# Attention scores masked by TensorE, minima by one VectorE instruction out of PSUM, exponentials straight from there

## The chip, the cores and the metric

The kernel runs on one core of one Trainium2 chip. The time is the device time of the program in microseconds (us). Engines are named as in the profile: PE is TensorE (PEld its weight loads), DVE is VectorE, ACT is ScalarE, POOL is GpSimd, SP is SyncE, which here issues most transfers.

## The reference, cut to what matters

The program is one attention layer, then a mixture of eight experts with one expert per token, then a two-layer product with a squared ReLU. The change touches the attention (and the sums of squares of its result, which the router needs):

```python
def _attn_ref(q, k, v):                        # 4 batches, 8 heads, 576 positions, 64 wide
    scores = scale * np.matmul(q, k.transpose(0, 1, 3, 2))      # scale = 1/8
    mask = (rel >= 0) & (rel < 64)             # a query sees itself and the 63 before it
    scores = np.where(mask, scores, -1e9)
    scores = scores - np.max(scores, axis=-1, keepdims=True)
    attn = np.exp(scores)
    attn = attn / (np.sum(attn, axis=-1, keepdims=True) + 1e-09)
    return np.matmul(attn, v)

def _moe_ref(x, ...):                          # x: 2304 tokens, 512 wide
    xn = x / (np.linalg.norm(x, axis=-1, keepdims=True) + 1e-06)
    logits = xn @ en.T / tau                   # argmax picks the expert, softmax gives the gate
    ...
```

## The kernel before, in words

**Steps.** The result of attention has 2304 rows, taken as 18 tiles of 128 tokens (t = 0 to 17). A tile holds two blocks of 64 queries (c = 0, 1), and a block needs 128 keys: its own 64 and the 64 before. Heads go in four pairs (hp); the two heads of a pair lie in the two halves of the partitions. `steps` is a list of 36 steps, each with two slots (t, hp). A step makes 2 slots x 2 heads x 2 blocks of scores, in a PSUM tile `spb` of two banks, one for each head: `spb[128, head, n % 2, slot, 128]`. The halves n % 2 alternate from step to step, and both lie in the same bank.

**Order.** PE's and SP's order is written by hand (the loop at L873): scores of step n, then pieces of `prep` (transposes of q and k for later steps), the flips of step n-2 (transposes of its exponentials), router work that is due (`run`), and the products with v of step n-3 (`fins`, and one step sooner from step 31 on). DVE, ACT and POOL are ordered by a planner that simulates the program; waits between engines follow from which instruction reads and writes which tile.

**One step's softmax.** `scores` (L234): 16 matmuls write q times k; four DVE instructions, one for each slot and head, add a mask from SBUF, scale by -1/8, write the sum to `sm` in SBUF and keep its minimum in `mn`. In steps 2 to 30 POOL then subtracts the minimum, and one ACT instruction takes exp(-x) over all 512 columns (L252, L259); in the others ACT makes four exponentials with the minimum as bias (L262). `flip` (L265) transposes by PE and copies back by ACT; `pv` (L273) multiplies with v, and DVE divides by the row sums (L283 to L289).

**Preparation.** `prep` (L216) turns k and q of one unit (a batch and a pair of heads) by PE into PSUM; each of its four pieces is copied out by two instructions, on ACT for both heads of k and head 0 of q, on DVE for head 1 of q (`TOACT`, L770). There are 16 units, so 64 pieces.

**Router.** When a tile's last product is done, `fin` (L656) puts on the list: the write of the tile to memory, `route_turn` (transposes, a copy by ACT, and the sum of squares, L379 to L383: by ACT for tiles below 16, by DVE for the last two), logits, and some steps later ranks, lists, `route_norm` on POOL (L449) and gates. `x2p` holds a buffer `xh` that the first expert's tokens use later.

Of the kernel before, what the change touches and what calls it, by code (L numbers as in the profile page):

```python
# [8 lines left out]
F32 = mybir.dt.float32  # L9
# [11 lines left out]
def tile_kernel(ctx, tc, q, k, v, emb, tau, w1, w2, w_in, w_out, s_in, b_in, out, x_dram, y_dram, y0_dram, wi_dram, wo_dram):  # L21
# [7 lines left out]
    QC = S // (2 * QP)  # L29
    BIG = 3.0e38  # L30

# [161 lines left out]

    mask = at.tile([128, 3, 128], F32, name="mask")
    nc.gpsimd.memset(mask, 0.0)
    for v_ in range(3):
        for h in range(2):
            m = mask[64 * h:64 * h + 64, v_]
            if v_ == h + 1:
                nc.gpsimd.affine_select(out=m, in_=m, compare_op=ALU.is_ge, fill=-8.0e9,  # L200
                                        base=0, pattern=[[-1, 128]], channel_multiplier=1)
                continue
            nc.gpsimd.affine_select(out=m, in_=m, compare_op=ALU.is_ge, fill=-8.0e9,
                                    base=-1, pattern=[[1, 128]], channel_multiplier=-1)
            nc.gpsimd.affine_select(out=m, in_=m, compare_op=ALU.is_ge, fill=-8.0e9,
                                    base=64, pattern=[[-1, 128]], channel_multiplier=1)

# [8 lines left out]
    def prep(b, hp):  # L216

        kt, qt = qk.pop((b, hp))
        n = (b * NP + hp) % NB
        for nm, src, dst in (("k", kt, kTs[n]), ("q", qt, qTs[n])):  # L220
            for h in range(2):
                pt = ps3.tile([128, QC, QP], F32, tag="tp", name="tp")
                for c in range(QC):
                    nc.tensor.transpose(pt[:, c], src[:, h, c], ident[:QP, :QP])
                for par in range(2):
                    o = dst[64 * h:64 * h + 64].rearrange("r (c p e) -> r e c p", c=QC, e=2)[:, par]
                    i = pt[64 * par:64 * par + 64]
                    if (nm, h) in TOACT:
                        nc.scalar.activation(o, i, AF.Copy)
                    else:  # L230
                        nc.vector.tensor_copy(o, i)
                yield

    def scores(n, slots):  # L234
        for s, (t, hp) in enumerate(slots):
            for c in range(2):
                u, i = unit(t, hp, c)
                k0 = max(i - 1, 0) * 64
                for h in range(2):
                    rows = slice(64 * h, 64 * h + 64)  # L240
                    nc.tensor.matmul(spb[64 * c:64 * c + 64, h, n % 2, s], qTs[u][rows, i * 64:i * 64 + 64],
                                     kTs[u][rows, k0:k0 + 128], start=True, stop=True)
        sm = at3.tile([128, 4, 128], F32, tag="sm", name="sm")
        mn = at3.tile([128, 4], F32, tag="mn", name="mn")
        for s, (t, hp) in enumerate(slots):
            m = mask[:, 1 if 2 * t % NW == 0 else 2 if (2 * t + 1) % NW == 0 else 0]
            for h in range(2):
                j = 2 * s + h
                nc.vector.tensor_tensor_reduce(out=sm[:, j], in0=spb[:, h, n % 2, s], in1=m, scale=-1.0 / 8.0,
                                               scalar=BIG, op0=ALU.add, op1=ALU.min, accum_out=mn[:, j:j + 1])  # L250
        if P0 <= n < PS:
            nc.gpsimd.tensor_tensor(sm, sm, mn.unsqueeze(2).to_broadcast([128, 4, 128]), op=ALU.subtract)  # L252
            return sm, None
        return sm, mn

    def exps(sm, mn):
        pe = at3.tile([128, 4, 128], F32, tag="pe", name="pe")
        if mn is None:
            nc.scalar.activation(pe, sm, AF.Exp, scale=-1.0)  # L259
            return pe  # L260
        for j in range(4):
            nc.scalar.activation(pe[:, j], sm[:, j], AF.Exp, bias=mn[:, j:j + 1], scale=-1.0)  # L262
        return pe
# [49 lines left out]
    zer = rp.tile([128, 1], BF16, name="zer")  # L313

    def add(out, a, b):
        nc.tensor.matmul(out, a, b, start=False, stop=True, skip_group_check=True)

# [53 lines left out]
    def route_turn(t, lp=None):  # L371
# [5 lines left out]
        marks.append(nc.scalar.activation(xt, tp, AF.Copy))  # L377
        sq = (lp or at).tile([128, DM], F32, tag="sq", name="sq")
        if t >= TL:  # L379
            nc.vector.tensor_tensor_reduce(out=sq, in0=xw, in1=xw, scale=1.0, scalar=0.0,  # L380
                                           op0=ALU.mult, op1=ALU.add, accum_out=ss[:, t:t + 1])
        else:
            nc.scalar.activation(sq, xw, AF.Square, accum_out=ss[:, t:t + 1])  # L383
        return xt

    def route_logits(t, xt):
        for c in range(ND):
            for o in range(0, 128, 64):
                add(lg[o:o + 64, t], xt[:, c, o:o + 64], enT[:, c])

    def block(kk, ln, a):
# [264 lines left out]
    def fin(slots, pT):  # L656
# [4 lines left out]
        ts_ = sorted({t for t, _ in slots})  # L661
        nt = len(ts_)

        def write():
# [104 lines left out]
    now = [0]  # L769
    TOACT = (("k", 0), ("k", 1), ("q", 0))  # L770

# [63 lines left out]

    P0, PS = 2, 31

# [457 lines left out]
```

## Time and profile before

| | |
|---|---|
| time | 839.34 us median of 3 runs (836.24 to 839.41) |
| profiled execution | 840.44 us, its span 838.7 us, mean granted clock 0.964 |
| PE busy | 788.7 us (94%), 6350 matmuls |
| DVE, ACT, POOL busy | 507.8 us (61%), 393.9 us (47%), 203.5 us (24%) |

The attention stage is the first 156 us or so of the span; the experts and the last products follow. PEclk of the page is the TensorE clock that was granted, as a share of 2.4 GHz; 0.5 is 1.2 GHz. Busy time counts an engine as busy while an instruction of it runs; an instruction's idle time before it stands in brackets with what ended it. The copies of exponentials back from PSUM have L270, the q and k copies L229 (ACT) and L231 (DVE).

### The profile page before, as it was taken

Reading aid. Unit: us, or ns where it says so; the run is one execution under the profiler, and the core shown is the slowest. Engines: PE = TensorE matmul, PEld = TensorE weight load, DVE = VectorE, ACT = ScalarE, POOL = GpSimd, SP = SyncE. Lnnn points to the kernel's source line nnn. Section 1 sums busy time; section 2 is a strip of 40 time slices with the busy share of each in tenths; the row PEclk is TensorE's granted clock in tenths of the full one; section 3 lists DMA queues with packets and bytes.
Section 4 is the critical chain, followed back from the end, with each engine's and each line's share of the span. In section 5 each row is a group of like instructions: output and inputs, shape, how many; then the busy total and the mean of one; then the engine's idle time right before and its main releaser. Section 6 shows DMA issues by size and latency. Waiting matters only on the chain.

```text
span 838.7 us, 16564 instructions
## 1 busy us (share of the span) xinstructions
PE 788.7 (94%) x6350; PEld 722.9 (86%) x6350; DVE 507.8 (61%) x1306; ACT 393.9 (47%) x796; POOL 203.5 (24%) x188
## 2 busy tenths in 40 slices
PE   6988887698999999899899999999999999999996
PEld 4776776598999999899899999999999999999885
DVE  3746586867777658689565555666655444444442
ACT  5866877414434545446354444445535333322331
POOL 3412335431112352444202222222210110101010
PEclk9967996889999999999899999999999999999999
DMA  8954846136849778677463332333324111100000
GB/s 186 216 150 125 217 131 213 73 119 201 238 154 317 230 250 270 219 243 273 163 218 111 101 101 101 100 114 107 121 89 124 53 38 39 51 26 26 27 26 26
DMA packets 100643, 117.16 MB, mean 140 GB/s; under 512 B 38885, under 2 KB 72165, under 8 KB 100561
## 3 DMA queue, kind: packets, MB, share of 16 engines
q1 hardware_dynamic: 91072, 99.11, 39.2%
q0 software_dynamic: 3232, 10.24, 3.5%
q10 hardware_dynamic: 6256, 6.72, 2.4%
q8 instruction: 51, 0.84, 0.4%
q14 instruction: 32, 0.25, 0.1%
HBM read 91.52 MB, written 24.53 MB: 138 GB/s over the span
## 4 chain that ended last, share of the span: by engine, by line
PE 50%; issue 0%; DMA 0%; POOLq 0%; DVE 0%
PE p L126 49%; PE tp L132 1%; DMA out_dram<-o,ids 0%; POOLq L1290 0%; DVE o L1240 0%; POOLq L1241 0%
## 5 line engine op out<-in xcount | busy, mean ns | idle before, releaser
L126 PE MATMUL p<-xl,wh 128*128 128x256 f32 x576 | 162.6, 282 | 0.0
L126 PE MATMUL p<-xh,wh 128*128 128x256 f32 x576 | 162.3, 282 | 0.0
L126 PE MATMUL p<-xh,wl 128*128 128x256 f32 x576 | 161.9, 281 | 0.0
L1202 ACT ACTIVATE r<-p 128x256 f32<-128x256 f32 x144 | 55.2, 384 | 168.5 <-PE p L126 162.3
L1203 DVE SCALAR_TENSOR_TENSOR r<-r,s_bc 128x256 f32<-128x256 f32 x144 | 79.5, 554 | 79.2 <-ACT r L1202 78.9
L126 PE MATMUL p<-wh,gh 128*128 128x512 f32 x288 | 113.1, 393 | 0.0
L126 PE MATMUL p<-wl,gh 128*128 128x512 f32 x288 | 113.1, 393 | 0.0
L126 PE MATMUL p<-wh,gl 128*128 128x512 f32 x288 | 113.0, 393 | 0.0
L126 PEld LDWEIGHTS p<-xh,wh 128*128 128x128 f32 x576 | 108.9, 189 | 0.7
L126 PEld LDWEIGHTS p<-xl,wh 128*128 128x128 f32 x576 | 108.7, 189 | 0.8
L126 PEld LDWEIGHTS p<-xh,wl 128*128 128x128 f32 x576 | 109.1, 189 | 0.0
L1026 POOL TENSOR_TENSOR fl<-fl,fs 128x512 f32<-128x512 f32 x32 | 45.9, 1438 | 253.1 <-DVE fs L1025 215.6
L88 DVE TENSOR_TENSOR wl<-raw,wh 128x1024 fp32r<-128x1024 f32 x72 | 102.5, 1432 | 7.0 <-ACT wh L87 6.9
L87 ACT ACTIVATE wh<-raw 128x1024 fp32r<-128x1024 f32 x80 | 83.3, 1056 | 7.9 <-DMA raw<-in_moe_w_dram 3.8
L126 PE MATMUL p<-hh,wh 128*128 128x256 f32 (+5 forms) x256 | 78.7, 308 | 0.0
L126 PE MATMUL p<-hl,wh 128*128 128x256 f32 (+5 forms) x256 | 77.0, 301 | 0.0
L126 PE MATMUL p<-hh,wl 128*128 128x256 f32 (+5 forms) x256 | 77.0, 301 | 0.0
L1209 ACT ACTIVATE gh<-r,b_bc 128x256 fp32r<-128x256 f32 x144 | 72.5, 503 | 7.4 <-DVE r L1203 7.4
L1210 DVE SCALAR_TENSOR_TENSOR gl<-r,b_bc,gh 128x256 fp32r<-128x256 f32 x144 | 71.2, 494 | 3.1 <-ACT gh L1209 3.1
L1241 POOL DMA_INDIRECT out_dram<-o,ids x18 | 18.6, 1035 | 203.7 <-DVE o L1240 182.5
L126 PEld LDWEIGHTS p<-wh,gl 128*128 128x128 f32 x288 | 54.1, 188 | 12.1
L126 PEld LDWEIGHTS p<-wh,gh 128*128 128x128 f32 x288 | 54.1, 188 | 11.4
(222 smaller groups left out, 1488.7 us busy)
## 6 DMA issues: line engine op xcount, KB each, us to landing
raw<-in_moe_w_dram SPq DMA_DIRECT2D x64, 512.0 KB, 4.8
raw<-y_dram SPq DMA_DIRECT2D x18, 512.0 KB, 3.8
vb<-in_v_dram SPq DMA_DIRECT2D x64, 128.0 KB, 3.7
fr<-in_moe_w_in_dram SPq DMA_DIRECT2D x16, 512.0 KB, 5.6
fr<-in_moe_w_out_dram SPq DMA_DIRECT2D x16, 512.0 KB, 4.2
k<-in_k_dram SPq DMA_DIRECT2D x32, 144.0 KB, 3.4
q<-in_q_dram SPq DMA_DIRECT2D x32, 144.0 KB, 3.6
x_dram<-xs SPq DMA_DIRECT2D x8, 512.0 KB, 3.2
```

What stands on the lines that cost most here:

```text
L87: a = nc.scalar.activation(hi, src, AF.Copy)
L88: return a.ins, le.tensor_tensor(lo, src, hi.bitcast(F32), op=ALU.subtract).ins
L126: nc.tensor.matmul(ps, a[x], b[y], start=first and j == 0, stop=last and j == 2)
L132: nc.tensor.matmul(ps, x, y, start=j == 0, stop=j == len(k) - 1)
L1026: nc.gpsimd.tensor_tensor(lf, lf, sg.bitcast(F32), op=ALU.mult)
L1202: nc.scalar.activation(r, ps, AF.Relu)
L1203: nc.vector.scalar_tensor_tensor(r, r, s_bc, r, op0=ALU.mult, op1=ALU.mult)
L1209: nc.scalar.activation(gh, r, AF.Identity, bias=b_bc)
L1210: nc.vector.scalar_tensor_tensor(gl, r, b_bc, gh.bitcast(F32), op0=ALU.add, op1=ALU.subtract)
L1241: nc.gpsimd.indirect_dma_start(out=out, out_offset=bass.IndirectOffsetOnAxis(ap=ids[:, k:k + 1], axis=0), in_=o, in_offset=None)
```

## The change

- The mask becomes a bf16 tile of 0 and 1e9. Before a step's score matmuls, PE writes it into PSUM with four matmuls by an identity of 64 (one for each block and head, 256 columns each), and the score matmuls add to it. The scale -1/8 is put on q when it is copied out of PSUM in `prep`.
- One DVE `tensor_reduce` takes the minima of all 512 columns of the step from PSUM. `sm` and POOL's subtraction go.
- ACT makes four exponentials of 128 columns in every step, reading the scores from PSUM with the minimum as bias.
- All q copies are on DVE (`TOACT` keeps k).
- The squares of tiles 0 to 10 are no longer ACT's: when a group of one or two tiles is done, `squares` on POOL multiplies it by itself and adds halves until one column is left, in the buffer `xh` of `x2p`.

```diff
--- before.py
+++ after.py
@@ -27,7 +27,6 @@
 
     QP = 96
     QC = S // (2 * QP)
-    BIG = 3.0e38
 
     E, _, F = w1.shape
     NTT = NT // 128
@@ -191,19 +190,24 @@
     load_v(*units[0])
 
 
-    mask = at.tile([128, 3, 128], F32, name="mask")
-    nc.gpsimd.memset(mask, 0.0)
-    for v_ in range(3):
-        for h in range(2):
-            m = mask[64 * h:64 * h + 64, v_]
-            if v_ == h + 1:
-                nc.gpsimd.affine_select(out=m, in_=m, compare_op=ALU.is_ge, fill=-8.0e9,
-                                        base=0, pattern=[[-1, 128]], channel_multiplier=1)
-                continue
-            nc.gpsimd.affine_select(out=m, in_=m, compare_op=ALU.is_ge, fill=-8.0e9,
-                                    base=-1, pattern=[[1, 128]], channel_multiplier=-1)
-            nc.gpsimd.affine_select(out=m, in_=m, compare_op=ALU.is_ge, fill=-8.0e9,
-                                    base=64, pattern=[[-1, 128]], channel_multiplier=1)
+    mask = at.tile([128, 4, 128], BF16, name="mask")
+    maskf = at.tile([128, 2, 128], F32, name="maskf")
+    nc.gpsimd.memset(maskf, 0.0)
+    for h in range(2):
+        m = maskf[64 * h:64 * h + 64]
+        nc.gpsimd.affine_select(out=m[:, 0], in_=m[:, 0], compare_op=ALU.is_ge, fill=1.0e9,
+                                base=0, pattern=[[-1, 128]], channel_multiplier=1)
+        nc.gpsimd.affine_select(out=m[:, 1], in_=m[:, 1], compare_op=ALU.is_ge, fill=1.0e9,
+                                base=-1, pattern=[[1, 128]], channel_multiplier=-1)
+        nc.gpsimd.affine_select(out=m[:, 1], in_=m[:, 1], compare_op=ALU.is_ge, fill=1.0e9,
+                                base=64, pattern=[[-1, 128]], channel_multiplier=1)
+    nc.vector.tensor_copy(mask.rearrange("p (v r) n -> p v r n", r=2), maskf.unsqueeze(2).to_broadcast([128, 2, 2, 128]))
+    eye = at.tile([128, 64], BF16, name="eye")
+    nc.vector.tensor_copy(eye[0:64], ident[0:64, 0:64])
+    nc.vector.tensor_copy(eye[64:128], ident[64:128, 64:128])
+
+    def add(out, a, b):
+        nc.tensor.matmul(out, a, b, start=False, stop=True, skip_group_check=True)
 
     def unit(t, hp, c):
 
@@ -225,41 +229,43 @@
                 for par in range(2):
                     o = dst[64 * h:64 * h + 64].rearrange("r (c p e) -> r e c p", c=QC, e=2)[:, par]
                     i = pt[64 * par:64 * par + 64]
+
+                    sc = 1.0 if nm == "k" else -0.125
                     if (nm, h) in TOACT:
-                        nc.scalar.activation(o, i, AF.Copy)
+                        nc.scalar.activation(o, i, AF.Copy, scale=sc)
+                    elif nm == "k":
+                        nc.vector.tensor_copy(o, i)
                     else:
-                        nc.vector.tensor_copy(o, i)
+                        nc.vector.tensor_scalar(o, i, sc, None, op0=ALU.mult)
                 yield
 
     def scores(n, slots):
+
+        sp = spb[:, :, n % 2]
+        first = [[(2 * t + c) % NW == 0 for t, _ in slots] for c in range(2)]
+        for c in range(2):
+            m0 = 2 - sum(first[c])
+            assert first[c] == sorted(first[c], reverse=True)
+            for h in range(2):
+                rows = slice(64 * h, 64 * h + 64)
+                nc.tensor.matmul(sp[64 * c:64 * c + 64, h].rearrange("p s n -> p (s n)"), eye[rows],
+                                 mask[rows, m0:m0 + 2].rearrange("p s n -> p (s n)"), start=True, stop=False, skip_group_check=True)
         for s, (t, hp) in enumerate(slots):
             for c in range(2):
                 u, i = unit(t, hp, c)
                 k0 = max(i - 1, 0) * 64
                 for h in range(2):
                     rows = slice(64 * h, 64 * h + 64)
-                    nc.tensor.matmul(spb[64 * c:64 * c + 64, h, n % 2, s], qTs[u][rows, i * 64:i * 64 + 64],
-                                     kTs[u][rows, k0:k0 + 128], start=True, stop=True)
-        sm = at3.tile([128, 4, 128], F32, tag="sm", name="sm")
-        mn = at3.tile([128, 4], F32, tag="mn", name="mn")
-        for s, (t, hp) in enumerate(slots):
-            m = mask[:, 1 if 2 * t % NW == 0 else 2 if (2 * t + 1) % NW == 0 else 0]
-            for h in range(2):
-                j = 2 * s + h
-                nc.vector.tensor_tensor_reduce(out=sm[:, j], in0=spb[:, h, n % 2, s], in1=m, scale=-1.0 / 8.0,
-                                               scalar=BIG, op0=ALU.add, op1=ALU.min, accum_out=mn[:, j:j + 1])
-        if P0 <= n < PS:
-            nc.gpsimd.tensor_tensor(sm, sm, mn.unsqueeze(2).to_broadcast([128, 4, 128]), op=ALU.subtract)
-            return sm, None
-        return sm, mn
-
-    def exps(sm, mn):
+                    add(sp[64 * c:64 * c + 64, h, s], qTs[u][rows, i * 64:i * 64 + 64], kTs[u][rows, k0:k0 + 128])
+        mn = at3.tile([128, 2, 2], F32, tag="mn", name="mn")
+        nc.vector.tensor_reduce(mn, sp, axis=AX.X, op=ALU.min)
+        return sp, mn
+
+    def exps(sp, mn):
         pe = at3.tile([128, 4, 128], F32, tag="pe", name="pe")
-        if mn is None:
-            nc.scalar.activation(pe, sm, AF.Exp, scale=-1.0)
-            return pe
         for j in range(4):
-            nc.scalar.activation(pe[:, j], sm[:, j], AF.Exp, bias=mn[:, j:j + 1], scale=-1.0)
+            s, h = j // 2, j % 2
+            nc.scalar.activation(pe[:, j], sp[:, h, s], AF.Exp, bias=mn[:, h, s:s + 1], scale=-1.0)
         return pe
 
     def flip(pe):
@@ -311,9 +317,6 @@
     lg = rt[:, 160:160 + NTT * E].rearrange("p (t e) -> p t e", e=E)
     ls = rt[:, 344:344 + 5 * E * KT].rearrange("p (v e k) -> p v e k", v=5, e=E)
     zer = rp.tile([128, 1], BF16, name="zer")
-
-    def add(out, a, b):
-        nc.tensor.matmul(out, a, b, start=False, stop=True, skip_group_check=True)
 
     em = rp2.tile([E, DM], F32, tag="xg", name="em")
     esq = rp2.tile([E, DM], F32, tag="xg", name="esq")
@@ -375,18 +378,28 @@
             nc.tensor.transpose(tp[:, c], xw[:, c * 128:(c + 1) * 128], ident)
         xt = (lp or at3).tile([128, ND, 128], F32, tag=f"xt{t}" if lp else "xt", name="xt")
         marks.append(nc.scalar.activation(xt, tp, AF.Copy))
-        sq = (lp or at).tile([128, DM], F32, tag="sq", name="sq")
-        if t >= TL:
-            nc.vector.tensor_tensor_reduce(out=sq, in0=xw, in1=xw, scale=1.0, scalar=0.0,
-                                           op0=ALU.mult, op1=ALU.add, accum_out=ss[:, t:t + 1])
-        else:
-            nc.scalar.activation(sq, xw, AF.Square, accum_out=ss[:, t:t + 1])
+        if t >= LATE:
+            sq = (lp or at).tile([128, DM], F32, tag="sq", name="sq")
+            if t >= TL:
+                nc.vector.tensor_tensor_reduce(out=sq, in0=xw, in1=xw, scale=1.0, scalar=0.0,
+                                               op0=ALU.mult, op1=ALU.add, accum_out=ss[:, t:t + 1])
+            else:
+                nc.scalar.activation(sq, xw, AF.Square, accum_out=ss[:, t:t + 1])
         return xt
 
     def route_logits(t, xt):
         for c in range(ND):
             for o in range(0, 128, 64):
                 add(lg[o:o + 64, t], xt[:, c, o:o + 64], enT[:, c])
+
+    def squares(t, n):
+        sq = x2p.tile([128, 1024], F32, tag="xh", name="sq").rearrange("p (s d) -> p s d", s=2)[:, :n]
+        nc.gpsimd.tensor_tensor(sq, xs[t], xs[t], op=ALU.mult)
+        c = DM // 2
+        while c >= 1:
+            o = ss[:, t:t + n].unsqueeze(2) if c == 1 else sq[:, :, :c]
+            nc.gpsimd.tensor_tensor(o, sq[:, :, :c], sq[:, :, c:2 * c], op=ALU.add)
+            c //= 2
 
     def block(kk, ln, a):
 
@@ -660,6 +673,8 @@
             return
         ts_ = sorted({t for t, _ in slots})
         nt = len(ts_)
+        if t < LATE:
+            squares(t, nt)
 
         def write():
             nc.sync.dma_start(x_dram[t * 128:(t + nt) * 128].rearrange("(s p) n -> p s n", p=128), xs[t])
@@ -767,7 +782,7 @@
             yield
 
     now = [0]
-    TOACT = (("k", 0), ("k", 1), ("q", 0))
+    TOACT = (("k", 0), ("k", 1))
 
     ROUTED = {3: ((0, 4), (4, 5, 6, 7, 9, 10, 11, 12, 14)),
               4: ((4, 9), (3, 4, 5, 6, 7, 8, 9, 10, 12)),
@@ -833,7 +848,7 @@
 
     AHEAD, RATE = 3, 2.4
 
-    P0, PS = 2, 31
+    PS = 31
 
     SOME = (1, 1, 0, 0, 1, 1, 4, 2, 1)
```

## Rows read from the trace of the kernel before

**Rows 1.** Windows view, 20 us stretches: length, PE, PEld, DVE, ACT, POOL busy, clock, DMA, GB/s.
```profile
100.00:120.00 20.00, 16.46 (x290) 13.25 (x287) 17.94 (x104) 14.03 (x31) 6.69 (x6) 1.00 0.66 163
120.00:140.00 20.00, 15.74 (x275) 12.82 (x273) 13.64 (x91) 13.69 (x32) 8.32 (x7) 0.82 0.40 143
140.00:160.00 20.00, 18.89 (x263) 16.96 (x264) 13.26 (x61) 13.94 (x33) 8.44 (x5) 0.84 0.54 184
160.00:838.00 678.00, 652.98 (x4403) 612.49 (x4401) 406.24 (x738) 279.27 (x542) 149.78 (x109) 0.99 0.40 132
```

**Rows 2.** Windows view, cut at the starts of score bursts (whole steps).
```profile
19.51:41.39 21.88, 21.37 (x346) 16.86 (x345) 16.41 (x94) 19.63 (x43) 8.54 (x13) 1.00 0.98 206
41.39:64.88 23.49, 21.16 (x251) 17.57 (x247) 11.84 (x64) 14.90 (x35) 5.41 (x6) 0.64 0.55 143
64.88:70.53 5.65, 5.07 (x93) 4.13 (x90) 5.25 (x36) 4.70 (x11) 1.04 (x1) 1.00 0.60 140
74.70:86.10 11.40, 11.12 (x107) 9.00 (x104) 5.22 (x26) 9.13 (x22) 2.08 (x2) 0.55 0.42 124
104.00:109.65 5.65, 5.45 (x102) 4.56 (x98) 5.42 (x37) 5.16 (x12) 1.23 (x2) 1.00 0.98 240
109.65:114.23 4.58, 2.33 (x43) 1.70 (x39) 4.54 (x17) 2.52 (x5) 2.25 (x2) 1.00 0.58 124
114.23:118.43 4.20, 4.20 (x84) 3.49 (x82) 3.40 (x23) 2.31 (x5) 1.43 (x3) 1.00 0.10 38
```

**Rows 3.** Timeline, one fast step's chain: start us, us, instruction [idle before, what ended it].
```profile
28.47 0.67 PE L241 MATMUL spb<-kT,qT 64*64 64x128 f32 x16
...
29.34 0.28 DVE L249 CUSTOM_DVE_ANT_0 sm<-spb,mask 128x128 f32<-128x128 f32 x1
...
30.18 0.08 DVE L249 DVE_READ_ACCUMULATOR2_ANT mn<- 128x1 f32 x1
30.40 1.04 POOL L252 TENSOR_TENSOR sm<-sm,mn 128x512 f32<-128x512 f32 x1 [1.85 <-DVE mn L249]
...
30.76 0.67 PE L241 MATMUL spb<-kT,qT 64*64 64x128 f32 x16
...
31.85 0.62 ACT L259 ACTIVATE pe<-sm 128x512 f32<-128x512 f32 x1
```

**Rows 4.** Groups by shape, 0 to 158 us: count | busy us, mean ns | idle before.
```profile
L252 POOL TENSOR_TENSOR sm<-sm,mn 128x512 f32<-128x512 f32 x29 | 30.7, 1057 | 71.2 <-DVE mn L249 54.9 <-DVE gt L468 4.4 <-DVE val L471 2.7
...
L231 DVE COPY qT<-tp 64x288 f32<-64x288 f32 x32 | 14.6, 457 | 2.2 <-PE tp L224 1.5
L229 ACT ACTIVATE qT<-tp 64x288 f32<-64x288 f32 x32 | 13.7, 428 | 1.3 <-PE tp L224 0.9
...
L383 ACT ACTIVATE sq<-xs 128x512 f32<-128x512 f32 x16 | 10.1, 628 | 1.5 <-DVE xs L289 1.2 <-DVE oh L410 0.2
...
L380 DVE CUSTOM_DVE_ANT_0 sq<-xs 128x512 f32<-128x512 f32 x2 | 1.4, 693 | 0.1
```

**Rows 5.** Timeline at the first two steps.
```profile
10.99 1.12 PE L241 MATMUL spb<-kT,qT 64*64 64x128 f32 x14 [2.00 <-DVE qT L231]
...
12.50 1.28 ACT L262 ACTIVATE pe<-sm,mn 128x128 f32<-128x128 f32 x4 [3.18 <-DVE mn L249]
...
13.02 0.08 DVE L249 DVE_READ_ACCUMULATOR2_ANT mn<- 128x1 f32 x1
...
13.16 1.13 PE L241 MATMUL spb<-kT,qT 64*64 64x128 f32 x16 [1.04 <-DVE mn L249]
```

**Rows 6.** Waits of PE, 0 to 158 us: in total, times, longest.
```profile
PE po L280 <- DVE xs L289: 5.1, 3, 2.3
...
PE tpx L375 <- ACT kT L229: 2.9, 4, 1.4
```

**Rows 7.** Timeline, a PE stall in the stretch from 41.39.
```profile
45.05 0.63 ACT L383 ACTIVATE sq<-xs 128x512 f32<-128x512 f32 x1
...
46.57 0.66 PE L375 MATMUL tpx<-ident,xs 128*128 128x128 f32 x4 [1.44 <-ACT kT L229]
```

## The prediction, made before the changed kernel was run

> **What bounds the kernel now.** I read the 20 us windows first [rows 1]. After 160 us PE is busy 652.98 of 678 us at clock 0.99: the experts and the last products are PE's own time, so a delay or a gain in the attention stage (the first 156 us, the only part the change touches) reaches the end one for one. Inside that stage I cut the windows at the starts of the score bursts [rows 2], so that each row is a whole number of steps. There are three kinds of stretch. From 19.51 to 41.39 there are eight steps at full clock, 2.74 us each, with PE busy 21.37 of 21.88: PE's own instructions set the pace; the three short rows that begin at 64.88, 104.00 and 114.23 (two steps each) are alike. From 41.39 to 64.88 (four steps) and 74.70 to 86.10 (two steps) PE is full too, but at a mean clock of 0.64 and 0.55, which is 1.2 GHz for most of it. And in 109.65 to 114.23 (one step) DVE is busy 4.54 of 4.58 and PE only 2.33: DVE sets the end.
>
> Then one fast step in the timeline [rows 3]: the scores start at 28.47, the four minima run from 29.34 to 30.26, GpSimd's subtraction from 30.40 to 31.44, and the exponential ends at 32.47, 4.0 us after the scores began. The next scores went out at 30.76, so this chain is longer than a step and hidden by it: the score tile has two halves, and once DVE has read one, nothing holds PE.
>
> **The wait that the change adds.** Step 1's scores write the half that no one has used yet, and their data were there; still PE stood 1.04 us and started at 13.16, just after step 0's last minimum, which reads the other half, ended at 13.10 [rows 5]. Both halves lie in the same two PSUM banks, so the order between reader and writer is kept by bank and not by half. Before, the last reader of a step is DVE's fourth minimum. After, it is ACT's fourth exponential, which reads the same tile. So the scores of step n+1 must wait for all exponentials of step n, and with them all that stands behind them in PE's order written by hand: transposes of q and k, flips, products with v, router matmuls.
>
> The Trainium skill has this as a rule: "PSUM — Partial Sum Buffer", section "PSUM bank collisions raise a hardware error", says to guard PSUM by bank and partition quadrant and not by address. The row agrees with it, with its 1.04 us. Guarded by address the sum below would lose its largest term and end near 840; by bank it ends near 849.
>
> The length of that chain at full clock, from rows 3 to 5: score start to DVE start 0.87; four mask matmuls 0.17 (a quarter of the 16 score matmuls' 0.67, which lie on the same four 64x64 tiles; ends 0 and 0.67); one reduction over 512 elements 0.69 (the square over 512 elements took 693 ns; ends: 0.46, the 288-element copy out of PSUM, and 0.92, the four minima now); to ACT 0.1; four exponentials 1.28 (as at 12.50); to PE 0.06. Together 3.17. In the fast stretch ACT is busy 19.63 of 21.88, and the exponential at 31.85 began 0.41 after its input; I add 0.13 for such queueing and take **3.3 us per step**, ends 3.17 and 3.6. Only steps shorter than that now are lengthened:
> - 19.51 to 41.39: 8 x 3.3 - 21.88 = 4.5
> - 64.88 and 104.00: 2 x (6.6 - 5.65) = 1.9
> - 114.23: 6.6 - 4.20 = 2.4
>
> That is **+8.8** (3.17 gives 7.0, 3.6 gives 13.0).
>
> **The rest, part by part.**
> - *Mask on PE.* In the fast steps it is inside the chain. In the six steps at low clock and about four others where PE is full it is on the path: 6 x 0.17 x 1.69 (the score burst takes 1.13 at low clock, 0.67 at full [rows 3, 5]) + 4 x 0.17 = **+2.4** (0 to 9.5 by the ends of the mask's cost).
> - *DVE.* 36 reductions in place of 36 groups of four save 36 x 0.23 = 8.3; 32 q copies come over from ACT, 32 x 0.457 = 14.6 (a scaling out of PSUM is taken at the copy's price; 0.42 to 0.50 would move this by 1.3) [rows 4]. DVE gets 6.3 us more in the stage, hidden by PE in most steps. It shows where DVE is the bound, in the step from 109.65: two copies more, one reduction shorter, **+0.7** (0 to 2). Queued behind a late reduction are the division by the row sums and, by that, the next products: PE already lost 5.1 us to this in three waits [rows 6].
> - *ACT.* 29 single exponentials of about 0.62 [rows 3] become 4 x 128 in 1.28: +19; it loses 32 q copies of 0.428 (13.7) and the squares of tiles 0 to 10, 11 x 0.63 = 6.9 without their read-outs [rows 4]. The total hardly changes, but the squares come in bunches: the one at 45.05 stands before the k copies for which the transposes at 46.57 waited 1.44 us [rows 7]. All waits of those transposes for k copies are 2.9 us [rows 6]. I take **-2.0**, ends 0 and -2.9.
> - *GpSimd.* It loses 29 subtractions of 1.06 [rows 4]. Their place in the chain gains nothing: no PE wait that I found ends with them, since flips come two steps later. It gains one product and nine halving sums for each of six groups of tiles: 4.2 us a group by elements at the subtraction's rate, 11.7 if each costs a whole one. The norm that needs them comes eight to ten steps later (five for tiles 9 and 10), over 16 us, and GpSimd stands idle more than half of the time [rows 1]. Cost 0; if that cover were gone, the gate's lists would be late, up to 2.
> - *Start.* The mask and a small identity are now needed by the first scores at 8.30, and go through DVE, which is waiting for a transfer then. The first scores already wait 2.00 us for one q half on DVE [rows 5]; with two halves there it may be 0.9 to 1.9 worse, or 2.0 better if the copies are put ahead of the router's setup. I take 0.
> - *SP.* No issue moves; loads that follow prep are later only as the steps are.
>
> Sum: 8.8 + 2.4 + 0.7 - 2.0 = **+9.9**. The profiled execution took 840.44 us (span 838.7 and 1.7 around it), 1.1 above the median of 839.34, and the sum is a difference within it: 839.3 + 9.9 = **849 us**.
>
> **Rivals.**
> 1. *The clock stays up: faster.* Each low-clock stretch comes after a PE stall, and the first stall has ACT's squares in it [rows 7]. With them gone, PE may stay at 2.4 GHz. From the mean clocks, low time is 2 x (1 - clock): 16.9 us in 41.39 to 64.88, 10.3 in 74.70 to 86.10 [rows 2], 7.2 + 6.4 in 120 to 160 [rows 1]. At 1.69 each gives back 41%: 6.9 + 4.2 + 5.6 = 16.7 at most, so 849.2 - 16.7 = 832.5; the first two alone give 838. It decides when all three stretches go, or two and half of the bank wait. For it: PE at 16.46 busy of 20 kept clock 1.0 in 100 to 120 [rows 1], and a fast step with 2.7 of 3.3 us busy is about that. Against it: the waits of 5.1 us on DVE [rows 6] stay, and DVE gets more to do.
> 2. *The new wait brings the clock down: slower still.* If the short idle time of each step costs the clock from 19.51 to 41.39, PE's 21.37 us become 36.1, with masks 38.4 in place of 26.4: 861. Against it the same row from 100 to 120.
> 3. *No bank wait* (the change doesn't do what I say): scores wait only for their own half, two steps back. Then masks cost 0.17 in some 14 fast steps more, 2.4, in place of 8.8: 843; if most of them fall into waits, 840. Against it: the 1.04 us of step 1, for which I see no other reason.
> 4. *Another order on DVE and ACT.* A planner orders these engines anew; a reduction put behind router work adds its time to every step that it delays. The waits on DVE were 5.1 us and could double or go: 844 to 854, inside the first case's range.
>
> **How the numbers follow.** Bank wait with the clock about as now: 0.55 with rival 4, own range 843 to 857 (the ends of the chain, the mask and the copies). Rival 1: 0.20. Rival 2: 0.12. Rival 3: 0.13. The range takes in rival 1's far end and the first case with its bounds, and rival 2 only in part: 833 to 861. Within 0.5%, which is about what a measurement here can tell from no change, is 835.1 to 843.5. Faster: most of rival 1 and a little of rival 3 and of a lucky order, 0.22. Same: the low edge of the first case, part of rivals 1 and 3, 0.19. Slower: 0.59.
>
> **What would show it.** Right: the score bursts of fast steps start 3.2 to 3.6 us apart, and the idle time before their first mask matmul ends with ACT's pe. The reduction takes 0.65 to 0.75 us and starts about 1.0 us after its scores; the four exponentials take 1.2 to 1.4 together; the mask matmuls add 0.1 to 0.3 to a burst; no transposes wait for ACT behind squares; GpSimd sums a group within 12 us and no norm waits for it. Wrong: fast steps at 2.5 to 2.9 us with no wait on pe (rival 3), a clock row of 1.0 from 40 to 60 and 70 to 90 (rival 1), or a clock of 0.5 inside 20 to 40 (rival 2).

## The result, and the profile after

The changed kernel takes **847.84 us** (median of 4 runs, 844.55 to 850.55) against 837.81 for the kernel before (4 runs, 836.24 to 839.41): ratio 1.0118, interval 1.0073 to 1.0163. It is slower, by 10.0 us of these medians. The profiled execution took 848.11 us, span 846.3, so 7.6 more than the span before. One execution in all that follows, the control's of 907.57 us in run 1, is a slow one by its lower granted clock (0.925) and is left out of the control's time.

In the attention stage the last product with v was divided by its row sums at 165.87 us in place of 156.20, 9.7 later; 2.1 of that came back in the experts' stage. Part of it is the clock there: from 400 to 440 us it was 0.83 and then 1.00 before and 0.97 and 0.95 now, so, by the prediction's 2 x (1 - clock), 3.2 us at low clock in place of 6.8. At the prediction's 41% that is worth 1.5 us, an estimate; the rest is open.

Windows view of the changed kernel, columns as in [rows 1], the stretches cut at the starts of score bursts as in [rows 2]:

```profile
20.64:29.37 8.73, 7.93 (x97) 6.36 (x97) 4.82 (x13) 4.94 (x15) 0.00 (x0) 1.00 0.59 145
29.37:49.62 20.25, 15.08 (x280) 12.82 (x280) 13.54 (x36) 14.92 (x43) 3.17 (x2) 1.00 0.70 173
49.62:64.76 15.14, 13.49 (x264) 11.49 (x264) 10.68 (x38) 12.13 (x34) 9.38 (x19) 1.00 0.76 204
64.76:73.13 8.37, 5.14 (x97) 4.44 (x97) 8.00 (x31) 5.52 (x15) 0.00 (x0) 1.00 0.69 152
76.61:86.71 10.10, 9.96 (x112) 8.31 (x111) 5.42 (x14) 6.30 (x18) 2.15 (x2) 0.62 0.34 109
104.99:113.34 8.35, 6.90 (x107) 5.99 (x106) 7.81 (x31) 5.09 (x16) 0.00 (x0) 0.81 0.99 204
113.34:116.69 3.35, 2.26 (x43) 1.85 (x43) 3.24 (x10) 2.06 (x6) 0.00 (x0) 1.00 0.01 1
116.69:122.90 6.21, 4.47 (x89) 3.82 (x89) 3.25 (x10) 3.30 (x11) 3.08 (x2) 1.00 0.23 87
134.20:145.12 10.92, 4.98 (x71) 4.24 (x70) 4.26 (x11) 6.38 (x12) 5.33 (x3) 0.71 0.70 251
```

The first two rows are the eight steps that took 21.88 us before: now 28.98, with PE busy 23.01 of them. PE was full there and is not any more. In the first of these two rows the score bursts take 1.12 and 1.07 us by themselves, as slow as before under a clock of 0.5 (1.13 at 48.91), though the row's granted clock reads 1.00; before, the burst at 22.06 took 1.16 as well. The third row is the stretch that ran at clock 0.64 and took 23.49: now clock 1.00 and 15.14. In the rows of 8.37 and 8.35 (two steps each, 5.65 before) DVE is the busy one, 8.00 and 7.81 us; the second of them also had a mean clock of 0.81. In the first, whose bursts start at 64.76 and 68.89, the reductions come late:

```profile
66.59 0.69 DVE L261 TENSOR_REDUCE mn<-spb 128x4 f32<-128x512 f32 x1
...
71.22 0.68 DVE L261 TENSOR_REDUCE mn<-spb 128x4 f32<-128x512 f32 x1
```

One fast step in the timeline, columns as in [rows 3]:

```profile
32.87 0.30 PE L251 MATMUL spb<-mask,eye 64*64 64x256 bf16 x4 [1.06 <-ACT pe L268]
...
32.98 0.63 PE L210 MATMUL spb<-kT,qT 64*64 64x128 f32 x16
...
33.75 0.69 DVE L261 TENSOR_REDUCE mn<-spb 128x4 f32<-128x512 f32 x1 [0.98 <-PE spb L210]
...
34.05 0.87 ACT L235 ACTIVATE kT<-tp 64x288 f32<-64x288 f32 x2 [0.74 <-PE tp L228]
...
34.93 1.14 ACT L268 ACTIVATE pe<-spb,mn 128x128 f32<-128x128 f32 x4
...
36.12 0.30 PE L251 MATMUL spb<-mask,eye 64*64 64x256 bf16 x4 [0.81 <-ACT pe L268]
```

Masks at 32.87, minimum ready at 34.44, exponentials 34.93 to 36.07, next masks at 36.12, of the other half of the score tile. The last exponential releases them. Between the minimum and the exponentials lie 0.49 us in which ACT still copies k.

Waits of the stage, 0 to 168 us, columns as in [rows 6]:

```profile
PE spb L251 <- ACT pe L268: 18.8, 19, 2.0
...
PE pt L274 <- ACT pT L276: 5.7, 1, 5.7
DVE nrm L470 <- POOL nrm L463: 4.5, 3, 2.9
PE po L286 <- DVE xs L295: 1.0, 1, 1.0
```

Groups by shape of the same stretch, columns as in [rows 4]:

```profile
L268 ACT ACTIVATE pe<-spb,mn 128x128 f32<-128x128 f32 x144 | 41.0, 368 | 15.5 <-DVE mn L261 12.1 <-DVE val L484 2.0 <-DVE gt L482 1.1
L239 DVE TENSOR_SCALAR qT<-tp 64x288 f32<-64x288 f32 x64 | 29.0, 454 | 2.9 <-PE tp L228 2.0
...
L261 DVE TENSOR_REDUCE mn<-spb 128x4 f32<-128x512 f32 x36 | 24.8, 688 | 17.4 <-PE spb L210 15.4 <-ACT pT L276 2.1
...
L397 POOL TENSOR_TENSOR sq<-xs 128x1024 f32<-128x1024 f32 x5 | 9.5, 1894 | 77.2 <-DVE xs L295 77.1
```

The prices of the prediction held: 688 ns for the reduction (forecast 0.69), 454 for a scaled q copy (0.457).

The one new stall that the forecast did not have, in the timeline at step 32:

```profile
138.55 1.06 ACT L86 ACTIVATE wh<-raw 128x1024 fp32r<-128x1024 f32 x1 [3.43 <-DMA raw<-in_moe_w_dram]
139.52 1.12 ACT L268 ACTIVATE pe<-spb,mn 128x128 f32<-128x128 f32 x4
...
141.18 1.12 PE L274 MATMUL pt<-ident,pe 128*128 128x128 f32 x4 [5.65 <-ACT pT L276]
```

In this program's order on ACT the copy of the first expert's weights comes ahead of step 32's exponentials. It waited 3.43 us for its transfer, the exponentials stood behind it, and PE 5.65 us behind them.

### The profile page after: what moved, and what is told of

Its sections match the earlier page's. It is cut to its first block, busy times and chain, and to the rows that moved or that the text cites. A ratio compares the mean times of both kernels' runs of the same rounds, so it can differ in the third digit from the quotient of the medians.

```text
span 846.3 us, 16671 instructions
## 1 busy us (share of the span) xinstructions
PE 784.0 (93%) x6494; PEld 722.6 (85%) x6494; DVE 512.9 (61%) x1089; ACT 387.3 (46%) x829; POOL 203.8 (24%) x215
## 5 line engine op out<-in xcount | busy, mean ns | idle before, releaser
L1256 POOL DMA_INDIRECT out_dram<-o,ids x18 | 18.4, 1022 | 204.2 <-DVE o L1255 182.7
```

The source lines that it names most:

```text
L1256: nc.gpsimd.indirect_dma_start(out=out, out_offset=bass.IndirectOffsetOnAxis(ap=ids[:, k:k + 1], axis=0), in_=o, in_offset=None)
```

## The experiments

Three theories at the start. **Chain:** scores wait for the last exponential of the step before, which reads the same PSUM banks. **Order:** the planner's new order on ACT and DVE, not the chain, costs the time. **Clock:** the squares' leave from ACT keeps PE's clock up and hides a larger loss. The expectations call the first one the bank theory, and set against it a load theory: the added work costs the time, and the wait only shows it. Ratios are against the kernel before, run in the same job.

**1 and 2. Halves in banks of their own.** The control gives up two PSUM banks first (flips share a ring of two buffers with the transposes), and the second kernel uses them to give each half of the score tile banks of its own. Each half is then a tile of its own, too.

```diff
 tp2:
-    ps3 = ap.enter_context(tc.tile_pool(name="ps3", bufs=3, space=PSUM))
+    ps3 = ap.enter_context(tc.tile_pool(name="ps3", bufs=2, space=PSUM))
-        pt = ps1.tile([128, 4, 128], F32, tag="pt", name="pt")
+        pt = ps3.tile([128, 4, 128], F32, tag="tp", name="pt")
 banks4, on top:
-    spb = ps1.tile([128, 2, 2, 2, 128], F32, tag="sp", name="spb")
+    spb = [ps1.tile([128, 2, 2, 2, 128], F32, tag=f"sp{i}", name="spb")[:, :, 0] for i in range(2)]
```

> A control for the next run: the changed kernel with the flips taken into the transposes' PSUM buffers and two of these instead of three, so that two banks stand empty. Bank theory (the scores of a step wait for ACT's exponentials of the step before, since both halves of the score tile lie in the same two banks): fast steps 3.3 to 3.8 us, PE's wait for pe before its mask matmuls still 15 us or more, time 847 to 856. Load theory (the loss is the added work on PE, DVE and ACT, and the wait only shows it): the same time.

> As the control, with the two halves of the score tile in banks of their own (four banks). Bank theory: PE's wait for pe falls from about 19 us to under 4, fast steps are 2.7 to 3.1 us, time 7 to 14 us under the control. Load theory: the wait moves to the flips or copies, fast steps stay at 3.2 or more, time within 2 us of the control.

Measured: control 903.94 us, ratio 1.0722 (1.0647 to 1.0796), far outside what I expected; own banks 885.57, 1.0543 (1.0525 to 1.056), 18.4 under the control. Waits of PE, first of the control (0 to 215 us), then of the kernel with own banks (0 to 196 us; no wait of the scores is left among them):

```profile
PE pt L274 <- ACT kT L235: 10.9, 12, 2.3
PE pt L274 <- DVE qT L239: 10.1, 9, 2.0
PE spb L251 <- ACT pe L268: 6.4, 5, 2.1
```

```profile
PE pt L274 <- DVE qT L239: 9.6, 9, 2.0
PE pt L274 <- ACT kT L235: 9.1, 12, 1.4
```

What follows: with own banks the wait for pe goes from 6.4 us to nothing, so it is the sharing that makes it. Whether the shared bank or the shared tile does, this pair can't tell, since the edit parts both. One row of the changed kernel, in the step shown above, says that the wait is coarser than a bank:

```profile
35.44 0.37 ACT L268 ACTIVATE pe<-spb,mn 128x128 f32<-128x128 f32 x1
```

This is the third exponential, the last one that reads head 0's bank, and it ended at 35.81; the first mask matmul writes head 0's bank, and it went out only at 36.12, after the fourth, which reads head 1's.

The size is not settled here either. The shared ring made new waits on the copies that free it, so that PE rarely reached the scores in time to wait for pe: the steps that are fast elsewhere take 3.28 to 3.92 us in both kernels, which is the load theory's sign and not the 2.7 to 3.1 of the bank theory. And 18.4 is more than 6.4. The control's rows come from an execution at a mean granted clock of 0.925, against 0.947 for the other kernel's, so they are read for their kind and not for their size; the control's execution at 0.945 took 893.02, some 7.5 over 885.57. The ring of transposes, at three buffers and without the flips, was worth some 56 us (903.94 - 847.84) by itself.

**3. A shorter chain.** One minimum for a partition's four rows, one exponential of 512 columns; the result stays a softmax.

```diff
-        mn = at3.tile([128, 2, 2], F32, tag="mn", name="mn")
-        nc.vector.tensor_reduce(mn, sp, axis=AX.X, op=ALU.min)
+        mn = at3.tile([128, 1], F32, tag="mn", name="mn")
+        nc.vector.tensor_reduce(mn, sp, axis=AX.XYZ, op=ALU.min)
...
-        for j in range(4):
-            s, h = j // 2, j % 2
-            nc.scalar.activation(pe[:, j], sp[:, h, s], AF.Exp, bias=mn[:, h, s:s + 1], scale=-1.0)
+        nc.scalar.activation(pe.rearrange("p (s h) n -> p h s n", h=2), sp, AF.Exp, bias=mn, scale=-1.0)
```

> The changed kernel with one minimum over the four rows that a partition holds (softmax is the same under any shift), and so one exponential of 512 columns in place of four of 128: 0.6 us in place of 1.14 in the chain. Bank theory: fast steps 2.75 to 3.0 us (from 3.25 to 3.5), PE's wait for pe under 8 us, time 836 to 842. Load theory: ACT has 18 us less to do, of which little is on the path: 844 to 848.

Measured 841.81 us, ratio 1.0023 (1.0005 to 1.0042): as expected in time, 6 us under the changed kernel (8 by the ratios). The wait for pe halved, to 9.7 us where I had said under 8. That wait, and a timeline of this kernel, two fast steps and one stall:

```profile
PE spb L251 <- ACT pe L266: 9.7, 15, 1.5
```

```profile
29.16 0.30 PE L251 MATMUL spb<-mask,eye 64*64 64x256 bf16 x4
30.17 0.69 DVE L261 TENSOR_REDUCE mn<-spb 128x1 f32<-128x512 f32 x1
...
31.38 0.69 ACT L266 ACTIVATE pe<-spb,mn 128x512 f32<-128x512 f32 x1
32.12 0.30 PE L251 MATMUL spb<-mask,eye 64*64 64x256 bf16 x4 [0.33 <-ACT pe L266]
...
33.72 0.69 ACT L266 ACTIVATE pe<-spb,mn 128x512 f32<-128x512 f32 x1 [1.16 <-DVE mn L261]
...
34.49 0.30 PE L251 MATMUL spb<-mask,eye 64*64 64x256 bf16 x4
...
55.06 0.17 DVE L468 TENSOR_SCALAR nrm<-nrm 128x4 f32<-128x4 f32 x1 [5.84 <-POOL nrm L461]
...
56.56 1.14 PE L284 MATMUL po<-vb,pT 128*64 128x65 f32 x16 [3.37 <-DVE xs L293]
```

Four exponentials took 1.14 us, one of the same 512 columns takes 0.69, so the chain loses 0.45 us, and steps come every 2.96 and 2.37 us in turn in place of 3.50 and 3.25. The steps lose more than the 0.45: in every second one the exponential now starts right behind the minimum, at 33.72, with the k copies after it, and PE doesn't wait for it any more. That part is order on ACT. The Trainium skill, "ScalarE: Activation LUTs", section "What ACT_TABLE_LOAD costs", gives an instruction with a bias operand 280 ns and 0.833 a column, less 93 for each that follows another; an estimate from that is 0.71 and 1.27. Both runs agree in kind; four measured 0.13 less. The last two rows are what came in place of the chain: in the faster stage GpSimd's squares are late, DVE, whose order is fixed, stood 5.84 us (and 5.29 once more, at 99.29) for a norm, and PE stood 3.37 us behind DVE.

**4. Exponentials first** in the planner's priorities (`tc.high_priority` around them).

> The changed kernel, with the exponentials given a higher priority in the planner, so that ACT makes them ahead of the copies of k and of the expert's weights. Bank theory: the exponentials start within 0.15 us of the minimum (now 0.5 to 0.75 later in fast steps), fast steps 2.95 to 3.15, and the stall of 5.7 us in step 32, where the exponentials stand behind a weight's copy, goes: 837 to 843. Load theory: the copies of k are late instead, only the stall goes: 843 to 846.

Measured 849.7 us, 1.0108 (1.0092 to 1.0125): a miss, and it says nothing of the chain. The planner left the exponentials where they were, behind the k copies (2.06 and 2.30 us after the burst's start, as in the changed kernel), and the stall of step 32 too.

**5. A longer chain.** The reduction is done twice (`for _ in range(2)` around it).

> The changed kernel with the reduction made twice, so that 0.69 us more stands between scores and exponentials. Bank theory: fast steps go from a mean of 3.37 to about 4.0, some 14 steps of this kind and a few others lengthened: 856 to 863. Load theory: DVE has 25 us more to do beside other work, fast steps at most 0.2 longer: 847 to 852.

Measured 885.38 us, 1.0538 (1.0505 to 1.0571). The waits of PE, 0 to 196 us:

```profile
PE spb L251 <- ACT pe L269: 32.5, 20, 2.8
```

Against 18.8 before the doubling: 13.7 us more, in the same place, about 20 x 0.69, and the five fast steps from 38.29 took 4.19 us on average, near the 4.0 that I expected. That part is the chain's. But the kernel lost 37.5 us, over twice what I expected; the rest I did not take apart. The clock is lower with it (0.88 and 0.72 from 40 to 80 us in place of 1.00 and 0.85).

**6. Squares back on ACT** (all tiles; POOL's sums go).

> The changed kernel with the squares of tiles 0 to 10 back on ACT. Theory that the squares' leave kept the clock up from 41 to 65 us: a low-clock stretch comes back near 45 to 65, transposes wait for copies of k, 852 to 860. Rival, that the even pace of the longer steps keeps the clock, or chance: no low clock there, 846 to 851, some 3 us of waits on ACT more.

Measured 849.01 us, 1.0109 (1.0081 to 1.0136). Windows, first the changed kernel, then this one:

```profile
40.00:60.00 20.00, 17.67 (x342) 15.15 (x334) 13.02 (x33) 15.62 (x44) 12.10 (x21) 1.00 0.80 208
```

```profile
40.00:60.00 20.00, 16.26 (x307) 13.91 (x306) 12.55 (x35) 17.54 (x49) 1.05 (x1) 1.00 0.72 193
```

The clock stays at 2.4 GHz with the squares on ACT as well. Moving them neither kept the clock up nor moved the time; the clock theory falls in that form. It falls only in that form, because the stall of the transposes behind the squares is not back in full: from 45 to 56 us they wait 0.8 us for k copies, and in the kernel before it was 1.44.

**7. The kernel before, with four exponentials** of 128 columns in all steps (POOL's subtraction goes; q's first head stays on ACT).

```diff
-    P0, PS = 2, 31
+    P0, PS = 99, 31
```

> The kernel before with one thing of the change alone: four exponentials of 128 columns in every step and no subtraction on GpSimd; they read the masked scores from SBUF, so the score banks are free after the minima. Bank theory: fast steps stay at 2.4 to 2.9 us and PE's wait for pe stays under 4 us, 835 to 844. Load theory (19 us more on ACT is what costs): fast steps over 3.1, 846 to 851.

Measured 844.25 us, 1.0057 (1.0024 to 1.0089). Windows and waits of this kernel:

```profile
20.00:40.00 20.00, 16.64 (x267) 12.77 (x263) 14.26 (x83) 19.54 (x52) 0.00 (x0) 1.00 0.77 188
```

```profile
PE pt L268 <- ACT pT L270: 9.1, 11, 2.3
```

The time lies between the two expectations, and the six steps from 25.48 took 3.12 us on average (2.65 before, 3.37 in the changed kernel), which is the load theory's sign. Here ACT is busy 19.54 of 20 us: the four exponentials cost 4.5 us (844.25 - 839.72) by ACT's load, with no wait of the scores for pe. In the changed kernel, whose ACT has no q copies, it is busy 13.42 of 20 in the same window. So I take it that there they cost by where they stand in the chain, not by filling ACT; what the two losses share can't be read from this run.

**8. One exponential, squares on ACT** (3 and 6 together).

> One minimum for four rows and one exponential, as before in this series, with the squares of tiles 0 to 10 back on ACT. In the run without that, DVE stood 5.3 and 5.8 us for a norm that waited for GpSimd's late squares. If these two stalls are what kept it from winning, they go and the time is 832 to 838; if ACT's squares bring the stalls of the transposes back, 839 to 844.

Measured 837.38 us, 0.998 (0.9942 to 1.0019), as expected, the lowest of all but not to be told from the kernel before. The two long waits for a norm are gone (4.3 us in four waits, longest 1.4). Step 32 still took 11.78 us. This run also bears on the clock. The next rows are windows in which PE did little, of the kernel before (with the 2 us that follow), then of run 3, then of run 8:

```profile
44.00:46.00 2.00, 0.78 (x6) 0.42 (x4) 0.14 (x1) 1.97 (x6) 0.15 (x1) 1.00 0.98 258
46.00:48.00 2.00, 1.43 (x22) 1.27 (x24) 1.03 (x2) 1.96 (x6) 1.92 (x2) 0.85 1.31 228
```

```profile
54.00:56.00 2.00, 0.00 (x0) 0.00 (x0) 0.81 (x5) 0.00 (x0) 1.03 (x1) 0.61 0.92 241
```

```profile
56.00:58.00 2.00, 0.19 (x7) 0.15 (x3) 1.89 (x7) 0.64 (x2) 0.00 (x0) 1.00 0.61 160
```

PE was busy 0.78, 0.00 and 0.19 us of the first 2 us shown of each. The clock fell at or right behind the first two and stayed at 1.00 at the third, until 66 us.

**9 and 10. The first weight copy on GpSimd**, alone and on top of 8.

```diff
-        a = nc.scalar.activation(hi, src, AF.Copy)
+        a = nc.gpsimd.tensor_copy(hi, src) if he else nc.scalar.activation(hi, src, AF.Copy)
...
-            hl, do = load_part(srcs[c], nc.gpsimd)
+            hl, do = load_part(srcs[c], nc.gpsimd, c < 1)
```

> One edit to the changed kernel: the high part of the first expert's first weight chunk is copied by GpSimd and not by ACT, so that step 32's four exponentials no longer stand behind a copy that waits 3.43 us for its transfer. Theory: that order is worth the 4.0 us that the stretch from step 32 to 33 grew by (6.93 to 10.91), so 843 to 845 in place of 847.8, PE's wait of 5.65 us before the flips under 2, and the rest of the steps as they were. Rival: the stall only stood in front of low clock or of a transfer that comes late anyway; then the stretch ends where it did: 846.5 to 848.5.

> The kernel with one minimum and one exponential of 512 columns and all squares on ACT (837.4) with the same copy given to GpSimd. Theory: its stretch from step 32 to 33 (11.78) loses 3 to 4 us as well: 833 to 835, faster than the kernel before. Rival: as for the run with that edit alone, 836.5 to 838.

Measured: alone 845.39 us (6 runs), 1.0081 (1.0051 to 1.0111), between the two expectations, and its interval overlaps that of the changed kernel. On top of 8: 838.73 (12 runs), 1.0015 (0.9993 to 1.0038), a miss. Timeline of the first:

```profile
137.48 1.14 ACT L268 ACTIVATE pe<-spb,mn 128x128 f32<-128x128 f32 x4 [1.83 <-DVE mn L261]
...
139.16 1.12 PE L274 MATMUL pt<-ident,pe 128*128 128x128 f32 x4 [3.11 <-ACT pT L276]
139.60 1.04 POOL L86 CAST wh<-raw 128x1024 fp32r<-128x1024 f32 x1 [11.78 <-DMA raw<-in_moe_w_dram]
```

The exponentials no longer stand behind the copy, PE's wait falls from 5.65 to 3.11, where under 2 was expected, and the step from 10.92 to 8.37 us. Its last product came 2.6 us earlier, but this execution's span (846.1) was only 0.2 shorter: what was won there was lost behind it, and I don't know where.

**11. q's first head back on ACT, in the kernel of 10.** (`TOACT` with `("q", 0)`.)

> As the run before this, and the 32 copies of q's first head back on ACT. With one exponential a step ACT has 0.5 us or more of room in a fast step, and DVE loses 32 copies of 0.45 us. Theory: DVE's reductions and divisions start earlier, in the steps in which DVE is behind above all: 0 to 3 us under that run, 830 to 834. Rival: the copies stand in front of the exponentials on ACT, which the next scores wait for: up to 32 x 0.2 = 6 us more in the fast steps, 835 to 840.

Measured 842.63 us (12 runs), 1.0054 (1.0029 to 1.0078), on the rival's side and past its range: 3.9 us over run 10. With one exponential a step, the copies stand in front of it on ACT, and the waits for pe grow from 9.8 to 16.0 us. Here the short chain needs the q copies on DVE.

**12. The same copies back on ACT, in the changed kernel.**

> One edit to the changed kernel: the 32 copies of q's first head go back from DVE to ACT. Theory (the chain from scores to the last exponential sets the fast steps, and its part on ACT is long by what stands in front of the exponentials): 20 or so more copies of 0.43 us in front of them, half of which adds to the chain, so fast steps of 3.5 to 3.8 us and 849 to 853. Rival (DVE is the late one: its copies of q stand in front of the reductions): steps of 3.0 to 3.2 and 842 to 846.

Measured 848.89 us, 1.0119 (1.0085 to 1.0154): no change from the changed kernel, and just under the theory's range. Timeline of ACT in a fast step of it:

```profile
32.22 0.87 ACT L235 ACTIVATE kT<-tp 64x288 f32<-64x288 f32 x2 [0.74 <-PE tp L228]
33.10 0.85 ACT L235 ACTIVATE qT<-tp 64x288 f32<-64x288 f32 x2
33.97 1.14 ACT L268 ACTIVATE pe<-spb,mn 128x128 f32<-128x128 f32 x4
```

In such a step two q copies lengthen the chain by their whole 0.85 (4.12 us in place of 3.25), as the theory has it. What gives this back lies elsewhere. Step 32 took 4.65 us in place of 10.92, since the weight's copy no longer stands ahead of its exponentials (the next step, behind such copies, took 7.40 in place of 5.47). The first two of the eight steps took 5.82 in place of 8.73, with score bursts of 0.63 and not of 1.12. And in the last three short steps, 2.80, 2.81 and 2.79 in place of 3.35, 3.11 and 3.10, the planner put the copy of the flips (0.6 us) behind the exponentials and not ahead of them. So the equal medians don't show that the copies cost nothing.

## Why the prediction was right, point by point

The forecast was 849 us, by +9.9 within one execution; the medians give +10.0, the two profiled executions +7.7. The mechanism that carried it is there. Its sizes were off in both directions, and the sum is partly luck.

- **Bank wait, +8.8 forecast: +14.5 in the same stretches.** Masks wait for ACT's pe in 19 places, 18.8 us, for the half of the tile that they do not write; runs 2, 3 and 5 remove, shorten and lengthen this wait. The Trainium skill's rule that the prediction cites, from "PSUM — Partial Sum Buffer", section "PSUM bank collisions raise a hardware error", to guard by bank and not by address, agrees with those 18.8 us in so far as the address does not decide. That the bank does, and not the tile, is not shown, since the 1.04 us of step 1 and run 2 fit both. Fast steps take 3.37 us (20.25 / 6) where 3.3 was forecast: exponentials shorter (1.14, not 1.28), queue longer (0.49 to 0.75 behind the k copies, not 0.13). Three places hold the other 5.7 us. The first two of the eight steps, whose score bursts still take 1.28 us with their masks and not 0.74, took 8.73 in place of 6.6: 2.1. The two-step rows took 8.37 and 8.35 in place of 6.6: 1.8 each. There DVE is the bound. In the first of them the reduction starts 1.8 and 2.3 us after its scores, behind the router's instructions (forecast: 0.87), and the whole chain starts later. This is the fourth rival's way; I had put its price inside the first case and not into the sum. The row at 116.69 gave +2.0 (forecast 2.4).
- **Clock, not in the sum: -8.35.** The stretch from 41.39 is at 1.00 now and took 15.14 in place of 23.49; that at 74.70 is nearly as it was (10.10 for 11.40, clock 0.62). In the first, PE's own time fell by 7.7 (21.16 to 13.49 us busy). The first part of rival 1 happened, but not by the squares alone: run 6 has them on ACT and the clock up. Nor is it simply that PE has more idle time: run 8, with PE busy 9.98 of 10.65 us ahead of that stretch, kept 1.00 from 40 to 60, run 3, also with 9.98 of 10.65, fell to 0.86. What differs is what stood right at the fall, a hole in PE's work; the windows stand at run 8. Before and in run 3 the clock falls with or right behind the hole, and in the changed kernel PE is busy for 1.19 us or more in every 2 us from 40 to 64. But run 8 has a hole as well and keeps the clock. That closing the hole kept the clock up is thus possible and not shown; what keeps it up is open.
- **Step 32, not in the sum: +4.0** (6.93 to 10.92). A copy that waits for a transfer, put ahead of the exponentials by the planner. Run 9 takes 2.5 of it away.
- **Start, 0 forecast: +1.1.** The fourth step began at 20.64 and not at 19.51: the masks of the three steps after the first wait 1.98, 0.41 and 0.77 us for pe. The sum priced that wait only from the fourth step on.
- **Masks, +2.4: not found as a term of its own.** They add 0.11 us at a burst's start, and the stretches where they should show grew by 0.4 (86.71 to 104.99) or shrank.
- **DVE, +0.7 in the step from 109.65:** it took 3.35 for 4.58, so -1.2; the copies hurt in the two-step rows instead.
- **ACT, -2.0:** the transposes' waits for k copies fell from 2.9 us to 0.2, as forecast in kind.
- **GpSimd, 0:** a group's squares and sums take about 5.7 us by the means of their rows, and DVE's wait for a norm was 4.5 (longest 2.9), much as before, though the prediction's sign was that no norm waits. Right in size here, but the cover is thin: in the faster stage of run 3 it was gone, at 5.84 and 5.29 us.
- **Rival 2** is out (clock 1.00 from 20 to 40 with PE at 15.63 of 20), and **rival 3** by the waits on pe.

By stretches: +14.5 - 8.35 + 4.0, and -0.5 for all others, make the 9.7 by which the last product is later. The prediction let a delay in this stage reach the end one for one; 2.1 of these 9.7 did not.

## What to carry to other kernels

When the reader of a double-buffered PSUM tile changes from the engine that reads first to the one that reads last, look whether both halves share a tile and its banks: then, as here, the next writer waits for the end of the whole chain, although it writes the other half. The length of such a chain includes what stands in front of each of its instructions on an engine whose order is fixed: price it by the queue at that moment, here 0.5 to 0.75 us of copies on ACT and up to 1.5 us of router work on DVE, not by the instruction. And a forecast whose sum is right can rest on two terms of 8 and 6 us that were missed with opposite signs; compare stretch by stretch before believing it.

## What I had not expected of the hardware

- One exponential of 512 columns out of PSUM takes 0.69 us, four of 128 take 1.14.
- Two PSUM buffers fewer for transposes and flips cost 56 us, more than five times the effect studied.
- PE at 98% busy and PE at 75% (15.08 of 20.25) both ran at 2.4 GHz in the same part of the stage. In run 3 the clock fell while PE stood for 3.37 us; in run 8 PE was busy 0.19 of 2 us and it stayed.
- A gain in the attention stage does not reach the end one for one: run 9 had its last product 2.6 us before that of the changed kernel and a span 0.2 shorter; run 8 had it 5.8 before that of the kernel before (150.4) and a span 4.0 shorter (834.7).
